# A seventh six-row group, one more sum by accumulating DMA, and a new written-out order in a WaveNet layer

## The chip, the cores and the metric

The kernel runs on one core of one Trainium2 chip. The metric is device time in microseconds (us) of one execution; lower is better. Engines are named as the profile names them: PE (TensorE), PEld (its weight loads), DVE (VectorE), ACT (ScalarE), POOL (GpSimd) and SP (SyncE, here only a DMA queue).

## The reference

```python
B, T, D, K = (2, 16000, 256, 3)          # all bfloat16
dil, pad = 2, 4
xp = jnp.pad(x, ((0, 0), (pad, 0), (0, 0)))
h  = sum over i of einsum('btc,cd->btd', xp[:, pad-2*i : pad-2*i+T, :], w[i])   # i = 0, 1, 2; d = 512
f, g = h[..., :256], h[..., 256:]
return (tanh(f) * sigmoid(g)) @ w_o
```

A causal convolution of three taps, two time steps apart, maps 256 channels to 512. Half of these go through tanh, half through a sigmoid, and the product of the two goes through a 256x256 matrix.

## The kernel before, in words

**Groups.** Each batch's 16000 time steps are cut into groups. A group of J rows holds J*R consecutive steps, laid out as J rows of R columns, so that the steps that a tap combines lie in different rows. Except for the first group (640 steps, kind P, computed tap by tap in `direct`, L406) the convolution is done with fewer products than taps, on sums and differences of rows:

- a four-row group (kind B, J = 4, R = 256: 1024 steps) takes four products, on the operands `m` and `p` (the sums at minus and plus one), `d0` (zero) and `d3` (infinity);
- a six-row group (kind A, J = 6, R = 256: 1536 steps) takes five, on `u1`, `rm` and `rp` (minus and plus one), `r0` (zero) and `ri` (infinity). Each of the last four is made in two steps: DVE makes `e`, `f`, `u0`, `u2` from the input tile and `u3`, `uh`, `ud` from `u1`; then `rm` is `e` plus `u3`, `rp` is `f` plus `u1`, `r0` is `u0` plus `uh` and `ri` is `u2` plus `ud`, written over `e`, `f`, `u0` and `u2`.

The As and Bs are numbered through both batches (A0 to A11, B0 to B12). `N_A = (6, 6)` gives the number of six-row groups in each batch; four-row groups take the rest, the last of them (B12) with R = 160.

**Blocks.** A group is computed in four blocks, one for each 128 of the 512 features, and each product is two matmuls (256 channels in two halves) of 2*R columns. The blocks stand in one sequence of 100 slots (`seq`, L180 to L188): four Bs first, then As and Bs mixed evenly, then two Bs.

For a block, PE makes the first product (F) in a PSUM bank, ACT copies it out (`c`, L432), PE adds the second (for A: M, then L; for B: L), and DVE combines the copy and the bank: `h` (halfway, A only, after M), `a` into a second PSUM bank and `y` into SBUF (A only), L435. PE then adds the products at zero (Z) to the first bank and at infinity (I) to the second. ACT applies tanh or sigmoid to the first bank (`b`), to `y` (A only) and to the second bank (`a`), L475. So a block costs ACT three instructions for a B and four for an A, and DVE one and three. DVE multiplies tanh by sigmoid (`g`, L494); PE multiplies by `w_o` in pieces of four matmuls (P, L512); ACT, at the very end DVE too (`v`), empties each piece into `osb` (`e`), and SP stores it (L540).

**The order.** Nothing is scheduled by a compiler: `PLAN` writes it out, one text line for each slot, from line -1 to line 104. A line has four parts: PE's letters, ACT's letters, DVE's letters and operands, and POOL's work. PE's F and M in line k are for block k, L for block k-1, Z and I for block k-2. H and R in the last lines are the output matrix's two halves for the last group. Every engine works through its own part in order and waits at semaphores.

POOL's part is put ahead of the line's `a` on DVE. A token there is a quarter of an operand (`d0`, `d3`, `r0`, `ri`, L382), a piece of the weights of six-row groups (`wa`, L299), or a whole `rm` or `rp`. Marks (`'`) name an earlier DVE instruction that a quarter is held behind. `rm` and `rp` are not computed on POOL; POOL issues an accumulating DMA for each:

```python
BY_DMA = ("rm", "rp")
...
if name in BY_DMA:
    return nc.gpsimd.dma_start(out=G[name][:, :, :, :R], in_=b, accum_op=op)
```

Input tiles (`xt`, four buffers for each kind) come by transposing DMAs from SP's queue (L234). A load stands in that queue at the end of the plan line that lies 15 slots ahead of the group's first (21 ahead for As), behind the stores of the lines before it.

Of the kernel before, what the change touches and what calls it, by code (L numbers as in the profile page):

```python
# [10 lines left out]


PLAN = """
 |  | d0.0 m.0 d3.0 p.0 G | 
F D D | c w |  | 
F L D | c d | m.1 a p.1 G | wa.1' wa.3'
F L Z I | c b | d0.1 a | wa.5' wa.0
L P F Z I | a e b c | a | wa.6
Z I F L P | a b c | d3.1 d3.2 d0.2 g a | wa.2
F L Z I | a c b | u1.0 e.0 a | wa.4'  # L20
L F Z I P | a c b | uh.0 g m.2 a | wa.14' wa.7' wa.8'
L P F Z I | a e e e b c | a | 
Z F P L I | a c b | u0.0 p.2 d3.3 u3.0 g a | wa.10 r0.0
L F Z I P | a e b c | u2.0 a | 
I F Z P L | a c b | ud.0 m.3 u2.1 g f.0 a | ri.0' r0.0'
L P F Z I | a e c b | a | 
Z L F I P | a b e c e | d0.3 u1.2 p.3 g f.1 a | rm.0 wa.15'
F L P Z I | a c b | d0.4 u1.1 d3.4 a | wa.12' wa.11
L F P Z I | a c e b e | a u3.1 m.4 g | wa.9
L Z F I P | a b c | u0.1 a | rp.0 r0.0'  # L30
F Z L I | a c b e | e.1 p.4 u3.2 a m.5 g | wa.13'
L F I Z P M | a c b | ud.1 a h | rm.1 r0.0' ri.0
F P Z L P I M | a e c e e b | g f.2 a y h | ri.0' ri.0 ri.1
F P Z L I | a e y b c | uh.2 u0.2 a y | d0.5' d3.5'
F L I Z M P | a c y b | uh.1 e.2 a h | r0.1' r0.2'
F I L Z M P | a c e e b | g a y h | rp.1 ri.1 r0.1
F Z L I | a y b c | g u2.2 a y | ri.1' d3.5'
F L I Z M P | c a y b | u1.3 ud.2 a h | r0.1' d0.5'
F Z L I M | a c b e | g a y h | rp.2 r0.1 ri.1
P F Z L I | a e y b c | e.3 ud.3 a y | rm.2 d0.5' d3.5  # L40
F L I Z M | a c y b | a p.5 h | d0.5 ri.2
Z I F L | a b c | g f.3 a y | r0.2' ri.2' d3.5'
F L P M P Z I P | c a e y b e e | g a h | ri.2
F L Z P M I | c a b e e | uh.3 u1.4 y u3.3 a h | ri.2' r0.2'
F Z L I P | a b c y | u3.4 u0.3 a y | d3.6' r0.2'
F L P Z I M | a e c b y | f.4 a g h | d0.6'
F I Z L P M P | c a b e | u2.3 uh.4 a y h | rp.3 rp.4 ri.3'' ri.3 d0.6''
F P Z L I | a e y e b c | g u0.4 a y | rm.3 d3.6' d3.6'
F P P Z L M I | a c e b e y | g m.6 a h | ri.3' r0.3
F Z L I | a b c | ud.4 e.4 a y | r0.3' ri.3'  # L50
F P L M Z I | c a y b | e.5 a h | d3.6' r0.3'
Z F I L P P M | a e b c e e e | u1.5 g p.6 a y h | rm.4 d0.6' r0.3' d0.6'
F P Z P L I | a c b y | g u2.4 a y | r0.4' ri.4 r0.4'
F L I Z M | a c y b | a m.7 h | ri.4
I F Z L P M P P | a e c b e | u0.5 g a h y | ri.4 d0.7
F L Z I P | a e e c b y | u3.5 a y | ri.4' d0.7'
F Z L I M | a c b y | e.6 uh.5 f.5 a h | d0.7' r0.4
F Z L I M P | a c e b | g a y h | r0.4 r0.5
F Z I L P P P | a e y c b e e e | u1.6 g a y | rp.5 d3.7
F L Z I M P P | a c y b | u3.6 u2.5 p.7 a h | r0.5' d0.7  # L60
Z F L I | a e b c | ud.5 g uh.6 a y | rm.5 ri.5' ri.5 r0.5'
F L I Z M P | a c e y b | f.6 a h | r0.5
Z F L I P M | a e b c e e | u0.6 u2.6 a y h | ri.5' ri.5'' d3.7''
F Z I L | a b c y | u1.7 g ud.6 a y | rm.6 d3.7' ri.6' d3.7' ri.6
F P L P M Z I | c a e y b | a h g | 
Z L F P I M P P | a c e e b e | f.7 a y h | rp.6 d3.8' d0.8' d3.8
Z P L F I | y a b c | u2.7 e.7 ud.7 a y | d0.8' r0.6''
F P L Z P M I | a e c y b e e | u3.7 g uh.7 a h | ri.7' r0.6'
F Z L P I | a b c e | u1.8 m.8 a y | r0.6' ri.6
F I L Z M P | a c y b | u0.7 g a h | rp.7 ri.6 d0.8 r0.6  # L70
F Z L M P I | a c b e e e | g a y h | ri.7 r0.7
F I Z L P | a c b y | u3.8 e.8 a y | d3.8
F P L Z M I | a c e b y | p.8 a h | rm.7 r0.7' d3.8'
F Z L P P M I | a e c b e e | u0.8 g a y h | ri.7 d0.8 r0.7 d0.9
F Z L I | a c b y | g a y | ri.7
L F I Z M P P | a c y b | f.8 uh.8 a h | rm.8 d3.9 d0.9'' r0.8'' r0.7''
F L P P M Z I | a e c e e e b | g y a h | d3.9
Z I L F | y b a c | u2.8 f.9 ud.8 y a | ri.8
F P L Z I M P | c y a b | e.9 u1.9 a h | ri.8' r0.8''
F Z L I | a c e b | g a y | rp.9 rp.8  # L80
L P F Z P M I | a c b y e | g u3.9 a h | r0.8' d3.9'
F I L Z M P | a c e b e | ud.9 u2.9 a y h | r0.8 ri.8'' d0.9''
I Z P L F | a e b y c | u1.10 uh.9 u0.9 a y | ri.8 d3.9 r0.9 r0.9
F P P L M Z I | c a e e b y | m.9 a h g | rm.9
Z F P L I P M | a c e b | f.10 a y h | d0.10' d0.9' ri.9'
F Z P L I | a y c b e | g p.9 a y | rp.10 r0.9' r0.9
F L I Z M | a c e b y | a ud.10 h u2.10 g | ri.9 d0.10
I F Z L P | a c b e e | a y | ri.9
L F P P Z M I | c a b y | uh.10 e.10 a h | ri.10' ri.9''
F Z I L P P M | a c e b e | u0.10 g a y h | d3.10 r0.10 r0.10  # L90
F Z I L P | a y b c | g a y | ri.10 ri.10
F L I Z M | a e c y b | u3.10 a p.10 h | r0.10'
Z P F L P I M P | a e e c b e e | g a y u2.11 h | rm.10 r0.10 d0.10 ri.10
Z F P L I P | y a c b e e | e.11 u1.11 a y | 
F L I Z M | a c y b | ud.11 a u3.11 h | d3.10'
Z P F L I M P | a b c e | m.10 g a y h | ri.11 d0.11
# [8 lines left out]
F P Z P L I | y a c b e e | a y | 
F L P Z M I | c a b y | p.11 a h g | d3.11' d3.12'
F Z L I | a c b e | a y | d3.12 d0.11
L F P P Z I | a y c e b | p.12 a g | d3.11'
L Z P F I | a b e c | m.12 a g | d0.12'
F Z L P I P | a c e e e b | a |   # L110
Z L I F P P P | a b e c e e | a g | d0.12
F I L P Z P | a c E b | a v | d3.12
I Z L P F | a b c | a g v | 
F Z I L P P | a c e b | a | 
# [9 lines left out]
def kernel(  # L124
# [13 lines left out]
    B, T, D = x.shape  # L138
    K, _, D2 = w.shape
    P = 128  # L140
# [13 lines left out]


    LEAD, TRAIL = 4, 1
    N_A = (6, 6)
    groups, of_kind = [], {"P": [], "A": [], "B": []}

    def group(kind, b, t, R):  # L160
        of_kind[kind].append(len(groups))
        groups.append(dict(kind=kind, b=b, t0=t, R=R, J=ROWS[kind]))
        return t + ROWS[kind] * R

    for b in range(B):
# [194 lines left out]
        return ins  # L360

    ON_TOP = {"rp": "f", "rm": "e", "r0": "u0", "ri": "u2"}
    BY_DMA = ("rm", "rp")

    def pre(g, name, eng, qs=slice(0, 4), behind=None):
        G = groups[g]
        R = G["R"]
        op, factor, a, b = operand(g, name)
        if name not in G:
            if name in ON_TOP:  # L370

                G[name] = G[ON_TOP[name]]
            else:
                pool = {"m": pre_pool, "p": pre_pool, "u3": sum_pool, "uh": sum_pool, "ud": sum_pool, "d0": dif_pool, "d3": dif_pool}.get(name, dif_pool)
                G[name] = pool.tile([P, 2, CT, RG], bf16, name=name, tag=name)
        if name in BY_DMA:
            return nc.gpsimd.dma_start(out=G[name][:, :, :, :R], in_=b, accum_op=op)
        o, a, b = (t if t is None else t.rearrange("p q ct r -> p (q ct) r")[:, qs] for t in (G[name][:, :, :, :R], a, b))
        if op is None:
            ins = eng.tensor_scalar_mul(o, a, factor)  # L380
        else:
            ins = eng.tensor_tensor(out=o, in0=a, in1=b, op=op)  # L382
        return hold(ins, behind)
# [185 lines left out]
    def gpsimd(tokens):  # L569
        for token in tokens:  # L570
# [5 lines left out]
            g, name = group_of(token)  # L576
            if name in BY_DMA:
                pre(g, name, None)
# [153 lines left out]
```

## Time and profile before

| | |
|---|---|
| median of three runs | 265.5 us (265.42 to 265.58) |
| the profiled execution | 266.35 us |
| its span, first to last instruction | 264.5 us |
| PE busy | 259.1 us (98%) |
| ACT busy | 244.2 us (92%) |
| DVE busy | 238.8 us (90%) |
| POOL busy | 143.8 us (54%) |
| mean granted PE clock | 0.996 |

The profile shows the profiled execution, which took 1.85 us more than its span and 0.85 us more than the median. The number of instructions of a kind stands behind an x, the mean duration of one in ns behind the comma; consecutive instructions of an engine overlap, so that durations add up to more than the engine's busy time.

### The profile page before, as it was taken

Reading aid. Unit: us, or ns where it says so; the run is one execution under the profiler, and the core shown is the slowest. Engines: PE = TensorE matmul, PEld = TensorE weight load, DVE = VectorE, ACT = ScalarE, POOL = GpSimd, SP = SyncE. Lnnn points to the kernel's source line nnn. Section 1 sums busy time; section 2 is a strip of 40 time slices with the busy share of each in tenths; the row PEclk is TensorE's granted clock in tenths of the full one; section 3 lists DMA queues with packets and bytes.
Section 4 is the critical chain, followed back from the end, with each engine's and each line's share of the span. In section 5 each row is a group of like instructions: output and inputs, shape, how many; then the busy total and the mean of one; then the engine's idle time right before and its main releaser. Section 6 shows DMA issues by size and latency. Waiting matters only on the chain.

```text
span 264.5 us, 4509 instructions
## 1 busy us (share of the span) xinstructions
PE 259.1 (98%) x1476; PEld 143.9 (54%) x1476; DVE 238.8 (90%) x396; ACT 244.2 (92%) x487; POOL 143.8 (54%) x209
## 2 busy tenths in 40 slices
PE   8999999999999999999999999999999999999993
PEld 5655555544455555465565545555555555555682
DVE  2999999999999999999999999999999997788372
ACT  4889989999999999999999999899999999999993
POOL 1034346668768775567858755758566266523100
PEclk9999999999999999999999999999999999999998
DMA  6999979839916793769447999856346436120425
GB/s 189 221 167 215 260 132 203 222 76 215 247 60 142 166 228 91 193 157 234 137 105 182 227 146 230 180 133 149 99 118 165 97 86 175 59 79 0 162 99 188
DMA packets 79583, 41.25 MB, mean 156 GB/s; under 512 B 68648, under 2 KB 69928, under 8 KB 79560
## 3 DMA queue, kind: packets, MB, share of 16 engines
q1 hardware_dynamic: 75060, 33.66, 51.7%
q0 software_dynamic: 3456, 6.29, 14.5%
q10 hardware_dynamic: 1044, 1.02, 1.2%
q8 instruction: 11, 0.18, 0.3%
q14 instruction: 12, 0.10, 0.1%
HBM read 1.25 MB, written 16.38 MB: 67 GB/s over the span
## 4 chain that ended last, share of the span: by engine, by line
PE 96%; ACT 2%; issue 0%; ACTq 0%
PE b L401 56%; PE o_ps L512 20%; PE a L401 16%; PE b L421 1%; PE a L421 1%; PE a L216 1%; ACT osb L537 1%; ACT sg L475 1%; ACT ss L432 0%; PE fill L248 0%; PE tp L308 0%; ACT th L475 0%; ACTq L432 0%
## 5 line engine op out<-in xcount | busy, mean ns | idle before, releaser
L435 DVE SCALAR_TENSOR_TENSOR a<-ss,b 128x512 f32<-128x512 f32 (+1 forms) x100 | 67.9, 683 | 10.6 <-PE b L401 5.6
L512 PE MATMUL o_ps<-wo_sb,zz 128*128 128x256 bf16 x496 | 70.9, 273 | 0.0
L537 ACT CAST osb<-o_ps 128x512 bf16<-128x512 f32 x118 | 69.6, 629 | 0.6 <-PE o_ps L512 0.4
L432 ACT COPY ss<-b 128x512 f32<-128x512 f32 (+1 forms) x100 | 60.5, 607 | 6.3 <-PE b L401 4.9
L512 PEld LDWEIGHTS <-zz 128*128 128x128 bf16 x496 | 48.5, 98 | 26.2
L382 POOL TENSOR_TENSOR d<-xt 128x256 bf16<-128x256 bf16 (+1 forms) x64 | 42.3, 668 | 35.5 <-DVE zz L494 12.9
L401 PEld LDWEIGHTS <-w_sb 128*128 128x128 bf16 x400 | 39.0, 98 | 39.6 <-issue 1.0
L382 POOL TENSOR_TENSOR u<-u,ud 128x256 bf16<-128x256 bf16 x48 | 35.7, 748 | 29.5 <-DVE zz L494 19.8
L382 POOL TENSOR_TENSOR u<-u,uh 128x256 bf16<-128x256 bf16 x48 | 38.4, 806 | 14.4 <-DVE zz L494 8.1
L494 DVE TENSOR_TENSOR zz<-th,sg 128x1024 bf16<-128x1024 bf16 (+2 forms) x52 | 41.5, 797 | 0.6 <-ACT sg L475 0.5
L435 DVE SCALAR_TENSOR_TENSOR hh<-ss,b 128x512 f32<-128x512 f32 x48 | 32.8, 682 | 3.0 <-PE b L401 2.4
L435 DVE SCALAR_TENSOR_TENSOR yy<-hh,b 128x512 f32<-128x512 f32 x48 | 32.6, 679 | 0.6 <-PE b L401 0.5
L475 ACT ACTIVATE sg<-b 128x512 bf16<-128x512 f32 (+1 forms) x50 | 31.1, 622 | 2.3 <-PE b L401 1.8
L475 ACT ACTIVATE th<-b 128x512 bf16<-128x512 f32 (+1 forms) x50 | 31.0, 620 | 2.2 <-PE b L401 1.7
L475 ACT ACTIVATE th<-a 128x512 bf16<-128x512 f32 (+1 forms) x50 | 31.3, 625 | 0.3 <-PE a L401 0.2
L475 ACT ACTIVATE sg<-a 128x512 bf16<-128x512 f32 (+1 forms) x50 | 31.3, 627 | 0.0
L401 PE MATMUL a<-d,w_sb 128*128 128x512 bf16 (+1 forms) x104 | 30.3, 373 | 0.0
L401 PE MATMUL b<-d,w_sb 128*128 128x512 bf16 (+1 forms) x104 | 30.3, 373 | 0.0
L401 PE MATMUL b<-m,wm_sb 128*128 128x512 bf16 (+1 forms) x104 | 30.1, 373 | 0.0
L401 PE MATMUL b<-p,wp_sb 128*128 128x512 bf16 (+1 forms) x104 | 30.1, 373 | 0.0
L401 PEld LDWEIGHTS <-wp_sb 128*128 128x128 bf16 x200 | 19.5, 98 | 19.1 <-issue 0.7
L401 PEld LDWEIGHTS <-wm_sb 128*128 128x128 bf16 x200 | 19.5, 98 | 16.8 <-issue 0.4
(57 smaller groups left out, 339.4 us busy)
## 6 DMA issues: line engine op xcount, KB each, us to landing
out_dram<-osb SPq DMA_DIRECT2D x24, 384.0 KB, 2.5
out_dram<-osb SPq DMA_DIRECT2D x26, 256.0 KB, 2.5
e<-u POOLq DMA_DIRECT2D x12, 256.0 KB, 4.3
f<-u POOLq DMA_DIRECT2D x12, 256.0 KB, 4.0
w_sb<-in_w_dram ACTq DMA_DIRECT2D x3, 256.0 KB, 4.0
xt<-in_x_dram SPq DMA_TRANSPOSE x25, 5.6
xn<-in_x_dram SPq DMA_DIRECT2D x1, 160.0 KB
xn<-in_x_dram ACTq DMA_DIRECT2D x1, 160.0 KB, 4.3
```

The costliest lines, as they stand in the source:

```text
L216: nc.tensor.matmul(wps[:], lhsT=ones[:, 0:P], rhs=ones, start=True, stop=True,)
L382: ins = eng.tensor_tensor(out=o, in0=a, in1=b, op=op)
L401: nc.tensor.matmul(G[bank, oi][:, :2 * R], lhsT=wmat[:, ct, osl], rhs=G[mv][:, :, ct, :R], start=which == "first" and ct == 0, stop=ct == ...
L421: nc.tensor.matmul(G[bank, oi][:, :4 * r].rearrange("p (j r) -> p j r", j=4), lhsT=w_taps[tap][:, ct, osl], rhs=xt[:, j0:j0 + 4, ct, c0 + ...
L432: nc.scalar.copy(out=G["ss", oi][:, :n], in_=G["b", oi][:, :n])
L435: return note(nc.vector.scalar_tensor_tensor(out=out, in0=in0, scalar=scalar, in1=in1, op0=ALU.mult, op1=op))
L475: nc.scalar.activation(out=G[name, dt][:, j:j + 2, :R], in_=G[bank, oi][:, :2 * R].rearrange("p (q r) -> p q r", q=2), func=(ACT.Tanh, ACT ...
L494: note(nc.vector.tensor_tensor(out=G["z"][:, dt, :, :n], in0=G["th", dt][:, :, :n], in1=G["sg", dt][:, :, :n], op=ALU.mult))
L512: nc.tensor.matmul(o_ps[:, q, :], lhsT=z, rhs=wo_sb[:, dt, :], start=dt == 0 and (q == 0 or len(dts) == NT), stop=dt == NT - 1, skip_group ...
L537: copy(out=osb[:, 2 * jp:2 * jp + 2, :], in_=o_ps[:])
```

## The change

```diff
-    N_A = (6, 6)
+    N_A = (6, 7)
...
-    BY_DMA = ("rm", "rp")
+    BY_DMA = ("rm", "rp", "r0")
```

In the second batch there are seven six-row groups (A0 to A12 in all). Four full four-row groups are left there instead of six, followed by one with R = 160 (B10, as B12 was) and a last one with R = 128 (B11). `r0` is made by an accumulating DMA, one for each group, instead of four quarters on POOL. The whole of `PLAN` is replaced. In the new one `m` and `p` of four groups, B5 to B8, are made by quarters on POOL instead of on DVE; the number of lines is the same (106). The counts of the tokens:

| | before | after |
|---|---|---|
| DVE: `a`, `h`, `y` | 100, 48, 48 | 100, 52, 52 |
| DVE: each of `u0 u1 u2 e f`, `u3 uh ud` | 12 | 13 |
| DVE: `m`, `p` | 13, 13 | 8, 8 |
| DVE: `d0`, `d3` | 5, 5 | 5, 5 |
| DVE: `v` (emptying pieces) | 6 | 4 |
| POOL quarters: `d0 d3`, `r0`, `ri`, `m p` | 64, 48, 48, 0 | 56, 0, 52, 32 |
| POOL's DMAs | 24 | 39 |

Lines of the new plan, with their numbers put ahead of them (the text after "SP:" tells which load the program puts at the end of line 52):

```text
52 F L P I M Z P | c a e y b | u1.8 a h | ri.6'               SP: load of B8
53 Z F I L P M | a b c e | u2.7 g a y h | d3.7 d0.7 p.8
54 P F Z P L I | a e y c b e e | g u3.7 ud.7 ud.8 uh.7 a y | rm.7 d3.7'' d3.7'' d3.7
55 F L P P M Z I | a c e e y b | a h | d3.8
56 Z L F I P M | a b c e | u0.8 u2.8 u3.8 a y h g | rp.7 p.8' ri.7 ri.8
...
63 L F Z I M | a c b | a y h | r0.8 ri.8 ri.8 d0.8
64 I Z F L | a y b c | u3.9 u2.9 a y | rp.9 m.8''
65 F P L I Z M | a c e y b | g a h | rm.9 m.8
```

The last lines, before and after:

```diff
-L Z I P p | a e b | g a v | 
-Z I P p P | a e b | v | 
-H H H | a e E | g v | 
-R R R |  |  | 
- | e E | v | 
+L Z I P | a e b | a g v | 
+Z I | a e b |  | 
+H H | a | g | 
+R R |  |  | 
+ | e | v | 
```

More of the change, by code (lines that the diff above doesn't have):

```diff
@@ L13 @@
 PLAN = """
- |  | d0.0 m.0 d3.0 p.0 G |
+ |  | p.0 m.0 d3.0 d0.0 G |
 F D D | c w |  |
[L16 to L36, printed above, removed]
@@ L105 @@
[L105 to L114, printed above, removed]
[L115 to L119 removed]
+F L D | c d | m.1 a G | wa.6
@@ new lines @@
+F L Z I | c b | a | wa.4
+L Z P F I | a b c | p.1 d0.1 a | wa.0'
+Z F L I | a b c | d3.2 d3.1 g a | wa.2
+F L Z I | a c b | u2.0 a | wa.1
+L Z I F P | a b e c | m.2 u1.0 a d0.2 ud.0 g | wa.3
+Z F I L | a b c | f.0 a | ri.0 wa.12'
+F P L Z I | a c e b e | p.2 a g | rp.0
+L F Z P I | a c b e | d0.3 a | wa.14
+L Z I F P | a b c | d3.3 u3.0 e.1 g a | wa.7
+F P L I Z P | a c e e b e | e.0 u1.1 a | wa.5'
+L P P Z I F P | a e e b c | uh.0 m.3 u2.1 > u0.1 a p.3 g | rm.0 wa.13'
+Z L F I | a b c | uh.1 d3.4 a | ri.0'
```

154 lines of the change are left out of this document (86 added, 68 removed).

## The prediction

> **What bounds the kernel now.** I read the page first, for the shares of the span and the chain that ended last.
>
> ```profile
> span 264.5 us, 4509 instructions
> ...
> PE 259.1 (98%) x1476; PEld 143.9 (54%) x1476; DVE 238.8 (90%) x396; ACT 244.2 (92%) x487; POOL 143.8 (54%) x209
> ...
> DMA  6999979839916793769447999856346436120425
> ...
> q0 software_dynamic: 3456, 6.29, 14.5%
> ...
> PE 96%; ACT 2%; issue 0%; ACTq 0%
> ```
>
> PE is 96% of the chain, but ACT and DVE are nearly as full. A busy PE need not be a PE at its pace, so the second view is the chain in order of time, which gives the pace, and the third the groups by shape, which give the number of matmuls.
>
> ```profile
> 5.28 3.08 PE b L421 x18
> ...
> 14.09 1.29 PE b L401 x6
> ...
> 58.18 1.46 PE b L401 x6
> ...
> 62.73 1.46 PE b L401 x6
> ...
> 248.24 1.31 PE o_ps L512 x12
> ```
> ```profile
> 255.31 0.54 PE b L401 x4
> ```
> ```profile
> L512 PE MATMUL o_ps<-wo_sb,zz 128*128 128x256 bf16 x496 | 70.9, 273 | 0.0
> ...
> L401 PE MATMUL b<-m,wm_sb 128*128 128x512 bf16 x96 | 28.5, 379 | 0.0
> ```
>
> An undisturbed matmul of 512 columns takes 1.29/6 = 0.215 us, one of 256 columns 1.31/12 = 0.109, one of 320 columns 0.54/4 = 0.135. There are nine groups of 96 like the second one here (864, 185.8 us), 500 of 256 columns (54.5) and 80 of 320 (10.8): 251.1 us. PE starts on real work at 5.28 us and issues its last matmul at about 259.8, so only some 3 us in 254.5 are not matmuls at full pace: 0.65 of it in the first 18 (3.08 instead of 2.43), and most of the rest in waits like those at 58.18 and 62.73, which make a run of six 0.17 us longer. PE's number of columns sets the time. The fourth view asks how near the others are, by stage.
>
> ```profile
> core 0: us, PE busy (x) PEld busy (x) DVE busy (x) ACT busy (x) POOL busy (x), PEclk, DMA share, GB/s
> ...
> 14.00:56.00 42.00, 42.00 (x228) 22.09 (x227) 41.58 (x74) 38.40 (x76) 21.44 (x32) 1.00 0.93 185
> 56.00:100.00 44.00, 43.91 (x240) 23.31 (x239) 43.66 (x74) 42.07 (x83) 32.64 (x44) 1.00 0.82 175
> ...
> 220.00:246.00 26.00, 26.00 (x147) 14.14 (x145) 19.69 (x31) 25.02 (x51) 10.39 (x18) 1.00 0.23 77
> 246.00:264.50 18.50, 13.95 (x110) 10.48 (x107) 8.74 (x18) 13.51 (x31) 0.90 (x2) 0.94 0.37 140
> ```
>
> DVE is full until 100 us (43.66 of 44, 0.59 us an instruction) and slack at the end; ACT is the second engine at the end (25.02 of 26, 0.49 us an instruction). POOL has room everywhere.
>
> **The change part by part: PE.** Two full four-row groups go: 2 x 4 products x 4 blocks x 2 halves = 64 matmuls of 512 columns, 13.76 us. A six-row group comes, 5 x 4 x 2 = 40 of them, 8.60 us, and the four-row group of R = 128, 32 matmuls of 256 columns, 3.49 us by the output product's pace. Steps and output product stay the same. Sum: **-1.67 us**, on the path that sets the end.
>
> **The end.** After the last block's product at infinity PE must wait for ACT's last activation and DVE's last gate before it can do R. These rows show the chain before.
>
> ```profile
> 257.11 0.43 PE L401 MATMUL a<-d,w_sb 128*128 128x320 bf16 x2
> ...
> 257.38 1.47 PE L512 MATMUL o_ps<-wo_sb,zz 128*128 128x256 bf16 x12
> ...
> 257.70 0.43 ACT L475 ACTIVATE sg<-a 128x320 bf16<-128x320 f32 x1
> ...
> 258.31 0.42 DVE L494 TENSOR_TENSOR zz<-th,sg 128x512 bf16<-128x512 bf16 x1
> ...
> 259.98 0.59 ACT L537 CAST osb<-o_ps 128x512 bf16<-128x512 f32 x1
> ```
>
> From the start of that product (257.11) to the end of the gate (258.73) 1.62 us pass, and PE is covered: three pieces (12 matmuls) and the H halves stand behind it. In the new plan only H H stands behind `Z I` in line 101: the product itself 0.22 and four matmuls 0.44, 0.66 us. Narrower tiles shorten the chain to an estimated 1.4 us (the odd piece's gate goes, each step has 256 instead of 320 columns), which leaves a hole of 0.74; ACT has an `e` ahead of the last two activations in each of lines 100 and 101, for which I add 0.15. **+0.9 us**, bounds 0.4 (nothing added, shorter steps) and 1.6 (both evictions, 0.59 each, half uncovered). After the last matmul one store remains instead of two; I cost that at nothing, since both were under way together.
>
> **DVE.** Durations overlap, so I use the pace of 0.59 and take shorter tiles off by the difference of these rows.
>
> ```profile
> L435 DVE SCALAR_TENSOR_TENSOR a<-ss,b 128x512 f32<-128x512 f32 x96 | 65.9, 691 | 8.0 <-PE b L401 4.6 <-ACT sg L475 2.3 <-ACT th L475 0.2
> ...
> L380 DVE TENSOR_SCALAR ud<-u 128x1024 bf16<-128x1024 bf16 x12 | 5.1, 426 | 0.0
> ...
> L435 DVE SCALAR_TENSOR_TENSOR a<-ss,b 128x320 f32<-128x320 f32 x4 | 2.0, 494 | 2.6 <-ACT th L475 1.5 <-PE b L401 1.0
> ```
>
> Four more `h` and `y`: +4.7. Four `a` become short (0.2 less or more each): -0.8. Operands of a group more: five at 0.59, three at 0.33 (426 against 691 ns): +3.9. `m` and `p`: ten fewer, -5.9, two shorter, -0.4. Two `v` fewer: -1.2. Gates: even. Sum +0.3 in 238.8, and by the plan's counts the surplus comes late, where DVE is slack; in the full first 100 us, where `m.5` to `p.6` leave it, it has about 1 us more room than before. I count nothing for that; it is worth at most the 2 us of waits that are there.
>
> **ACT.** Eight full blocks of three give way to four of four and four short ones of three, and two pieces come from DVE: -24 + 16 + 2 = -6 instructions of 0.49 us, and 12 short ones at an estimated 0.3: +0.7 us. Behind ACT's room in the page (20 us) that is nothing; at the end, where it has 1 us in 26, it comes off the rest: by counting, lines 83 to 104 hold as much ACT work as PE work, where before ACT had over 3 us less. Bounds 0 and +1 us beside the hole above; I take 0, because ACT at 25.02 of 26 cost PE nothing there (26.00 of 26.00).
>
> **POOL and the DMAs.**
>
> ```profile
> L382 POOL TENSOR_TENSOR d<-xt 128x256 bf16<-128x256 bf16 x56 | 38.6, 696 | 23.0 <-DVE zz L494 7.0 <-DVE yy L435 6.8 <-DVE e L382 3.2
> L382 POOL TENSOR_TENSOR u<-u,uh 128x256 bf16<-128x256 bf16 x48 | 38.4, 806 | 14.4 <-DVE zz L494 8.1 <-DVE u L382 4.5 <-DVE uh L380 0.7
> L382 POOL TENSOR_TENSOR u<-u,ud 128x256 bf16<-128x256 bf16 x48 | 35.7, 748 | 29.5 <-DVE zz L494 19.8 <-DVE yy L435 4.7 <-DVE u L382 3.4
> ...
> L494 DVE TENSOR_TENSOR zz<-th,sg 128x1536 bf16<-128x1536 bf16 x24 | 22.9, 952 | 0.0
> ...
> L377 POOL DMA_DIRECT2D e<-u x12 | 10.5, 877 | 0.0
> ```
> ```profile
> DMA to landing us min/median/max: 3.3/4.2/5.6
> ```
>
> POOL loses 48 quarters of `r0` (38.4 us, the second row) and 8 of `d` (5.6), and gains 32 of `m` and `p` (0.70 each, 22.3), four of `ri` (3.0) and 15 issues (0.88 each, 13.2): -5.5 us, and it sits off the path. What matters is lateness. An accumulating DMA landed 3.3 to 5.6 us after its issue (the last line is the view of the line that issues them). By the plan the shortest way from PE's start of a line with `r0` to the matmul that reads it is 5.6 us (`r0.8`: line 63, 2.15; line 64, 1.72; F, a piece, L and I of line 65, 1.73); the next are 6.1 (`r0.3`) and 6.5. So typical landings are covered and only the longest is not. Price 0, bounds 0 and +1. The queue q0 goes from 14.5% to 14.5 x 39/24 = 23.6% of the DMA engines; they are at 0.93 in the stretch from 14 to 56 us, but only two of the 15 DMAs fall there.
>
> A rule of the Trainium skill speaks against this part: by "SBUF — State Buffer", section "SBUF: two separate sides", GpSimd cannot write a DMA's descriptors while DVE holds the port that they share, so that such a DMA seems blocked. The DMAs here were issued beside a DVE that was 98 to 99% busy, and landed in 3.3 to 5.6 us; if that holds for the new ones the rule is in the numbers already.
>
> **Sum.** -1.67 + 0.9 = -0.77 us: 266.35 becomes 265.6 for a profiled execution. Carried to the median shown, which lies 0.85 lower, 265.5 becomes **264.7 us**.
>
> **The rivals.** *More room* (15%): PE's waits in the middle go, since DVE has the room, and the hole at the end is at its lower bound: -1.67 + 0.4 - 0.7 = -2, 263.5 us. For it: the waits are short and DVE was full where they are. Against: the plan is another, and brings its own.
>
> *Nothing gained* (14%): ACT, without room in the last 40 us, delays copies and banks by another 0.7 us: 265.4.
>
> *Late loads hold POOL* (25%), the one that ends slower. The load of B8 stands at the end of line 52, and `p.8`, which reads it, in line 53; B10 (line 77, read in 78) and B7 (39, read in 41) are like it.
>
> ```profile
> 147.66 2.27 SPq L234 DMA_TRANSPOSE xt<-in_x_dram  x1
> ```
> ```profile
> DMA to landing us min/median/max: 3.6/5.6/9.0
> ```
>
> The rows are the nearest load before, of B9, which stands in line 56 and was first read in line 59, and the landings of all (the view of the tile `xt`). POOL works in order: while `p.8` waits, `rm.7`, three quarters of `d3.7` and `rp.7` wait behind it. From the end of line 52, PE reaches the product that reads `d3.7` after line 53 (2.6 us), line 54 (2.6), line 55 (3.0) and three products (1.3): 9.5 us. POOL needs 0.7 + 0.9 + 2.1 = 3.7 after the landing, so a landing later than 5.8 us after line 52 decides. With the median of 5.6 it just does; with the longest PE waits 3.2 us. SP may issue earlier, because the last store ahead of that load belongs to line 50; that is why I do not take this as likeliest. Two such places at about 1 us: -0.77 + 2 = +1.2, 266.7 us.
>
> *Late sums* (4%): the skill's rule as a mechanism: an issue is held for one more gate, 0.95 us (952 ns above), on top of the longest landing, 6.6 us, and `r0.8`, `r0.3` wait 1.0 and 0.5: -0.77 + 1.5 = +0.7, 266.2 us. No landing in the profile speaks for it.
>
> **How the numbers follow.** A measurement of this kernel can tell about 0.2%, 0.5 us, from no change: below 265.0 is faster, above 266.0 slower. The forecast has 42%; within its own bounds (hole 0.4 to 1.6) it reaches from 264.2 to 265.4, and about a fifth of that I put within 0.2%. Faster: 34 + 15 = 49%. Same: 8 + 14 = 22%. Slower: 25 + 4 = 29%. The range goes from the "more room" case with 1 us of the waits gone, 263.2, to the late loads with 2.3 us at their places, 267.0.
>
> **What would show it.** Right: PE has 1476 - 64 + 72 matmuls (1484) and the same pace; a hole of near 1 us on PE ahead of the last four matmuls, ended by DVE's gate; no `u<-u,uh` on POOL and 39 DMAs that land in under 6 us; DVE near 239 us, ACT near 245, POOL near 138. Wrong: POOL idle for microseconds ahead of a `p` or `d` and released by a load, with PE's waits in the products behind; waits of PE on DMAs at Z of an A block; or runs of six matmuls that take over 1.29 us all through the last 40 us, released by ACT.

## The result and the profile after

The changed kernel takes **269.2 us** (median of four runs, 267.8 to 274.5) against 265.5 us on the same chip (265.3 to 265.6): ratio **1.0106, 95% interval 1.0079 to 1.0133**. It is slower by about 1.1%; 264.7 was forecast. The profiled execution took 268.24 us, its span 266.5 against 264.5. Ratios here leave out runs over 1.5% above a kernel's fastest; since late transfers make some runs of the changed kernel longer than that, I give the spread of all runs beside them.

The page of the kernel after, the lines that answer to those of before:

```profile
span 266.5 us, 4558 instructions
...
PE 257.4 (97%) x1484; PEld 143.5 (54%) x1484; DVE 243.4 (91%) x400; ACT 245.0 (92%) x493; POOL 140.1 (53%) x204
...
q0 software_dynamic: 5616, 10.23, 23.5%
...
PE 84%; ACT 6%; DVE 5%; issue 2%; ACTq 1%
```

The counts are as forecast (1484 matmuls, 23.5% for the queue, ACT 245.0). Two things are not: DVE is busy for 243.4 us instead of 239, and the chain that ended last went from 96% PE to 84%, with DVE and ACT in the gap. The view of PE's waits (what was waited for: us in total, times, longest) held only the warm-up line (`PEq`) for the kernel before. Now it has these:

```profile
PE b L401 <- DVE yy L435: 1.3, 2, 1.2
PE a L216 <- PEq L716: 0.8, 1, 0.8
PE b L401 <- DVE hh L435: 0.7, 1, 0.7
PE o_ps L512 <- DVE zz L494: 0.7, 1, 0.7
PE b L401 <- ACT ss L432: 0.7, 1, 0.7
PE a L401 <- DVE a L435: 0.5, 1, 0.5
```

`o_ps` waiting for `zz` is the forecast hole at the end. The other waits for DVE and ACT are new. From the starts of all matmuls and their undisturbed pace (0.2159, 0.1360 and 0.1093 us for 512, 320 and 256 columns), the two spans compare so: PE reaches the plan's first product at 10.93 us instead of 11.81 (-0.88); the matmuls from there on are worth 244.67 us instead of 246.36 (-1.69; forecast -1.67); waits among them come to 6.61 us instead of 1.61 (+5.00); from the end of the last matmul to the end of the span it is 4.24 us instead of 4.74 (-0.50). Sum +1.93, the measured difference. The first of these differences is not the change's: in the other profiles below the first product comes at 10.8 to 11.9 us with the new plan and at 11.1 to 11.4 with the old one.

Of the 6.61 us, 0.85 is the hole at the end, 0.83 a wait at 37.5 us that begins with a store, and about 4.4 lie between 50 and 180 us, 3.1 of it in four waits that DVE ends (at 66.6, 80.3, 148.0 and 173.8 us).

**Where DVE lost time.** The timeline of the kernel after around line 54 (start, duration; DVE, then POOL, then PE):

```profile
144.01 0.76 DVE L380 TENSOR_SCALAR ud<-u 128x1024 bf16<-128x1024 bf16 x2
144.68 2.10 DVE L380 TENSOR_SCALAR uh<-u 128x1024 bf16<-128x1024 bf16 x1
146.71 0.68 DVE L435 SCALAR_TENSOR_TENSOR a<-ss,b 128x512 f32<-128x512 f32 x1
...
144.40 0.88 POOL L377 DMA_DIRECT2D e<-u  x1 [1.32 <-DVE u L380]
145.01 1.48 POOL L382 TENSOR_TENSOR d<-xt 128x256 bf16<-128x256 bf16 x2
...
148.03 0.59 PE L401 MATMUL b<-u,w_sb 128*128 128x512 bf16 x2 [1.16 <-DVE yy L435]
```

`uh.7` takes 0.42 us elsewhere and 2.10 here. Behind `rm.7` POOL has run two quarters of `d3.7`, and DVE stands still until both are over; `a` and `y` come late, and PE waits 1.3 us for `y`. The Trainium skill says on the page "SBUF — State Buffer", section "SBUF: two separate sides", that DVE and GpSimd share a port pair as an exclusive lock, which goes to whichever starts first "for the whole instruction". The trace agrees that one waits for the whole of the other; who came first is less plain, since by the records `uh.7` starts 0.33 us ahead of the first quarter (144.68 against 145.01).

Five more places are like it. DVE took 1.93 us instead of 0.95 for `g` of line 24, 1.76 instead of 0.67 for `u2.9` (line 64), 1.2 instead of 0.7 for `u0.2` (19), for `g` and for `u1.4` (29), 1.34 instead of 0.94 for `g` (30). Over all DVE instructions, what they took beyond the shortest of their form (where that is over 80 ns) sums to **6.1 us; before, 1.3** (the expectations below count one of them less, 5.6). All of them read and write SBUF alone. `a`, `h` and `y`, which read PSUM, were never longer by more than 26 ns, though most of them ran beside a quarter; and of some 35 SBUF operations that overlapped only the issue of a DMA, the worst lost 0.15 us.

What POOL is doing as the DVE operation starts decides who pays. In the three largest places (`uh.7`, `u2.9`, `g` of line 24) POOL was issuing a sum at that moment, here `rm.7` from 144.40 us, with a quarter queued right behind. Over all 17 profiles 50 DVE operations lost more than 0.2 us, and each of them started while POOL had a quarter or a piece of the weights (35) or such an issue (15) under way. In 397 cases in which POOL was at none of these and a quarter started during the operation, DVE lost at most 0.02 us, and in most of them the quarter grew instead.

**Where the transfers lost time.** Answers on the tiles `xt` and `f` of the kernel after (the load issued at 25.4 us, `rp.0` at 26.1 us, and the landing of each behind its issue), and the wait on ACT that followed:

```profile
L234 SPq DMA_TRANSPOSE xt<-in_x_dram x1: 4236/4236/4236, 25.4 to 25.4; - x1
...
DMA to landing us min/median/max: 9.3/9.3/9.3
```
```profile
L377 POOL DMA_DIRECT2D f<-u x1: 1004/1004/1004, 26.1 to 26.1; - x1
...
DMA to landing us min/median/max: 8.4/8.4/8.4
```
```profile
35.34 1.07 ACT L537 CAST osb<-o_ps 128x512 bf16<-128x512 f32 x2 [0.85 <-DMA out_dram<-osb]
```

Before, sums landed in 3.3 to 5.6 us. Here the load and the first sum both took over 8 us, the next store came late behind them, and ACT waited for that store's buffer. The new plan issues `rp.0` in line 8 instead of line 15.

### The profile page after: what moved, and what is told of

Its sections match the earlier page's. It is cut to its first block, busy times and chain, and to the rows that moved or that the text cites. A ratio compares the mean times of both kernels' runs of the same rounds, so it can differ in the third digit from the quotient of the medians.

```text
span 266.5 us, 4558 instructions
## 1 busy us (share of the span) xinstructions
PE 257.4 (97%) x1484; PEld 143.5 (54%) x1484; DVE 243.4 (91%) x400; ACT 245.0 (92%) x493; POOL 140.1 (53%) x204
## 3 DMA queue, kind: packets, MB, share of 16 engines
q0 software_dynamic: 5616, 10.23, 23.5%
## 4 chain that ended last, share of the span: by engine, by line
PE 84%; ACT 6%; DVE 5%; issue 2%; ACTq 1%
PE b L401 50%; PE o_ps L512 17%; PE a L401 14%; ACT sg L475 2%; ACT th L475 2%; ACT osb L537 1%; PE b L421 1%; PE a L421 1%; DVE a L435 1%; ACT ss L432 1%; DVE hh L435 1%; DVE zz L494 1%; DVE yy L435 1%; ACTq L256 1%; ACT L267 0%
## 5 line engine op out<-in xcount | busy, mean ns | idle before, releaser
L435 DVE SCALAR_TENSOR_TENSOR a<-ss,b 128x512 f32<-128x512 f32 (+2 forms) x100 | 67.0, 671 | 10.7 <-PE b L401 5.4
L432 ACT COPY ss<-b 128x512 f32<-128x512 f32 (+2 forms) x100 | 59.2, 593 | 5.1 <-PE b L401 4.2
L382 POOL TENSOR_TENSOR d<-xt 128x256 bf16<-128x256 bf16 (+2 forms) x56 | 34.2, 626 | 37.2 <-DVE zz L494 24.4
L494 DVE TENSOR_TENSOR zz<-th,sg 128x1536 bf16<-128x1536 bf16 (+2 forms) x52 | 42.8, 823 | 0.8 <-ACT sg L475 0.5
L401 PE MATMUL b<-u,w_sb 128*128 128x512 bf16 x104 | 30.9, 379 | 1.4 <-DVE yy L435 1.3
L401 PE MATMUL b<-f,wp_sb 128*128 128x512 bf16 x104 | 30.9, 379 | 0.7 <-DVE hh L435 0.7
L401 PE MATMUL a<-u,w_sb 128*128 128x512 bf16 x104 | 30.9, 379 | 0.5 <-DVE a L435 0.5
L401 PE MATMUL b<-u,wa_sb 128*128 128x512 bf16 x104 | 30.9, 379 | 0.0
L475 ACT ACTIVATE sg<-a 128x512 bf16<-128x512 f32 (+2 forms) x50 | 30.9, 618 | 0.0
L401 PE MATMUL b<-e,wm_sb 128*128 128x512 bf16 x104 | 30.9, 378 | 0.0
```

The source lines that it names most:

```text
L401: nc.tensor.matmul(G[bank, oi][:, :2 * R], lhsT=wmat[:, ct, osl], rhs=G[mv][:, :, ct, :R], start=which == "first" and ct == 0, stop=ct == ...
L432: nc.scalar.copy(out=G["ss", oi][:, :n], in_=G["b", oi][:, :n])
L435: return note(nc.vector.scalar_tensor_tensor(out=out, in0=in0, scalar=scalar, in1=in1, op0=ALU.mult, op1=op))
L475: nc.scalar.activation(out=G[name, dt][:, j:j + 2, :R], in_=G[bank, oi][:, :2 * R].rearrange("p (q r) -> p q r", q=2), func=(ACT.Tanh, ACT ...
L494: note(nc.vector.tensor_tensor(out=G["z"][:, dt, :, :n], in0=G["th", dt][:, :, :n], in1=G["sg", dt][:, :, :n], op=ALU.mult))
```

## The experiments

Each ratio is to the kernel before on the same chip in the same batch. Its median there was 266.2 us for experiments 1 to 4, 266.1 for 5 to 8, 266.3 for 9 to 12 and 266.4 for 13 to 15, not the 265.5 of the first comparison; so ratios can be compared across batches, and times less well.

My theory after this: (A) quarters that meet DVE's SBUF operations cost some 4 us; (B) the early sum beside a load costs 0.8 us and more, by chance. Rivals: the denser mix of six-row groups is too much for DVE by itself; the sums by DMA are dear in themselves.

### First four

**1. Quarters moved away from DVE's SBUF operations.** Fifteen lines of POOL's part, no other:

```diff
18 -r0.1 ri.0' ri.1 d3.5' ri.1 ri.1' m.5       +r0.1 ri.0' ri.1 d3.5'
19 -                                           +ri.1'' ri.1'
21 -rp.1 p.5                                   +rp.1 p.5 m.5
24 -rm.2 p.5                                   +rm.2
26 -                                           +p.5'
28 -rm.3 m.5 ri.2 ri.3 d0.5 ri.3               +rm.3 m.5 ri.2 ri.3
29 -ri.2'                                      +ri.2 d0.5
30 -d3.5' d3.6' m.6'                           +d3.5'' d3.6'
31 -ri.3                                       +ri.3 ri.3
32 -d0.6'                                      +d0.6' m.6
54 -rm.7 d3.7'' d3.7'' d3.7                    +rm.7 d3.7 d3.7
55 -d3.8                                       +d3.7 d3.8
64 -rp.9 m.8''                                 +rp.9 m.8
69 -ri.9 d3.9 d0.9                             +ri.9 d3.9
70 -                                           +d0.9
```

> Only 15 lines of POOL's part of the new plan differ: quarters that ran beside a VectorE operation that reads and writes SBUF alone are put beside its PSUM operations, one or two lines later or with fewer marks. All counts, PE's, ACT's and VectorE's parts stay. Theory (a GpSimd quarter and a VectorE operation on SBUF shut each other out): the sum of what VectorE's operations take over the shortest of their kind falls from 5.6 us to under 1.5, VectorE's u from xt goes back from 743 to about 690 ns, PE's waits at 65, 80, 148 and 174 us go, and 3.5 to 4.3 us are won: profiled about 264.3, below the kernel before. Rival (the denser mix of six-row groups is too much for VectorE by itself): VectorE still 243 us busy, PE still waits 4 us in the first 180 us, 268. Rival (more traffic by accumulating DMAs): no change, 268.

Measured: 268.6 us (266.9 to 271.2), ratio 1.0087 (1.0056 to 1.0118). DVE's excess fell from 6.1 to 0.8 us, its busy time to 238.7, and none of the waits at 65, 80, 148 and 174 us is left; but the time hardly moved. Three views of its profiled execution (271.2 us) show why: the timeline, PE's granted clock (the whole span in 40 slices) and the DMA engines (19 us from 26 us on in 40 slices):

```profile
41.64 1.01 PE L401 MATMUL b<-p,wp_sb 128*128 128x512 bf16 x2 [3.94 <-ACT ss L432]
42.45 1.06 PE L401 MATMUL b<-m,wm_sb 128*128 128x512 bf16 x2
...
46.71 0.81 PE L401 MATMUL b<-d,w_sb 128*128 128x512 bf16 x2
47.36 0.59 PE L401 MATMUL a<-d,w_sb 128*128 128x512 bf16 x2
```
```profile
PEclk9999995999999999999999999999999999999999
```
```profile
DMA  9999996699999999999999999799999999679999
GB/s 249 236 285 247 116 45 31 31 185 287 223 39 39 158 63 74 161 73 120 121 77 149 58 146 66 169 397 385 276 233 213 350 311 323 175 167 118 85 200 182
```

The load took 12.8 us to land and `rp.0`, issued 0.4 us behind it, 11.8; in several slices the DMA engines count as 60% busy or more while 31 to 45 GB/s pass. The stores came late, ACT waited, PE stood still for 4.1 us, and for the 5 us after that each matmul took twice its time (1.06 us a pair instead of 0.59, starts 0.43 apart instead of 0.22), about 2.8 us more. On that the Trainium skill ("TensorE: Matmul & The Clock Gate", Part 1: "The HAM clock gate") says that an idle window of about 3.4 us halves the array's clock until such a window has been busy; the rows agree, with half the pace behind a wait of 4.1 us, though it lasted 5 us. So the harm of (B) was not 0.8 us in this run but near 7.

**2. The kernel before with `r0` by DMA, alone.** In `before`, for each of the 12 groups:

```diff
-    BY_DMA = ("rm", "rp")
+    BY_DMA = ("rm", "rp", "r0")
10 -ri.0' r0.0'                                +ri.0'
...
```

> The kernel before with one part of the change alone: each r0 by one accumulating DMA, issued where the first of its four quarters stood; the other 36 tokens are taken out. PE's, ACT's and VectorE's work stays. Theory (the harm is in where quarters lie beside VectorE, and the DMAs are in time): 265.4 within 1 us, POOL down by 28 us (48 quarters of 0.81 less 12 issues of 0.88), the queue's share at 22%, and whatever PE loses lies where a VectorE operation on SBUF meets a quarter. Rival (the DMAs' traffic or lateness): slower by 2 us or more, with PE's waits at the products at zero ended by DMAs, or with later landings of loads and stores.

Measured: 271.6 us (267.4 to 273.7). This went the rival's way. The profiled run (273.7) shows one place, the tiles `u` and `xt` at 28 us, and PE's waits:

```profile
L377 POOL DMA_DIRECT2D u<-uh x1: 1007/1007/1007, 28.1 to 28.1; - x1
...
DMA to landing us min/median/max: 11.5/11.5/11.5
```
```profile
PE b L401 <- DVE p L382: 4.4, 1, 4.4
PE b L401 <- DVE hh L435: 1.1, 1, 1.1
```

`r0.0` is issued 0.24 us behind a load; they land after 11.5 and 11.9 us, DVE's `u1.2` waits for that load with `p.3` queued behind it, PE waits 4.4 us for `p.3` and runs at half pace after it. At 100.3 us the same happens (`rm.4` 0.23 us behind a load, 9.1 and 9.7 us; PE waits 1.1). The rival's word "dear in itself" is not settled by this: experiment 9.

**3. A piece moved into the hole at the end.**

```diff
 99 -F I Z L P P        +F I Z L P
101 -Z I                +Z I P
```

> The kernel after with one piece (four matmuls of 256 columns) moved in PE's part from line 99 to the end of line 101, so that it stands between the last products and the last eight matmuls. Theory (a hole of 0.85 us before the last four matmuls): the hole shrinks by the piece's 0.44 us and the end comes 0.3 to 0.45 us earlier, 267.8 profiled. Rival (ACT has no room at the end, so a later piece only delays the last evictions): no gain or 0.3 us slower.

Measured: 273.9 us (272.7 to 275.9). Much of this is the early wait again (3.2 us at 40.6 in the profile, and half pace), which this edit has nothing to do with; one run was profiled, and why all six are long is not known. The end is read from the trace alone, and the rival is right:

```profile
265.86 0.39 ACT L475 ACTIVATE sg<-b 128x256 bf16<-128x256 f32 x1
...
267.04 0.61 PE L512 MATMUL o_ps<-wo_sb,zz 128*128 128x256 bf16 x4 [1.05 <-DVE zz L494]
```

The piece is finished later, its eviction on ACT stands ahead of the last two activations, and the hole grows from 0.85 to 1.22 us.

**4. A fourth output buffer.**

```diff
+    osb4_pool = ctx.enter_context(tc.tile_pool(name="osb4", bufs=4))
-            G["osb", rb0] = osb_pool.tile(...
+            G["osb", rb0] = (osb4_pool if J == 4 else osb_pool).tile(...
```

> The kernel after with a fourth buffer for the four-row groups' output tiles (osb), nothing else. Theory (ACT waited 0.85 us at 35 us for an older store to land, and PE lost 0.83 us at 37.5 us behind it): both waits go and the end is 0.8 us earlier, 267.4. Rival (the wait only covers another one, VectorE's collisions behind it absorb the gain): the wait goes, the waits of the next 20 us grow by as much, no change.

Measured: 269.7 us (267.3 to 274.5), ratio 1.0123 (1.0095 to 1.0152). The profiled run (267.28) has neither wait, and its span is 1.0 us shorter than that of the kernel after; but there the load and `rp.0` landed after 7.2 and 4.7 us, so the buffer was not put to the test, and other runs are as long as without it. Inconclusive.

### Second four: the place of the first sum

**5. The kernel before with its first sum early.**

```diff
 8 -wa.10 r0.0          +wa.10 r0.0 rm.0
12 -rm.0 wa.15'         +wa.15'
```

> The kernel before with one token moved: its first accumulating DMA (rm.0) is issued in line 8 instead of line 12, at about 29.4 us, so that it is under way together with the transposing load issued at 28.25. Theory (an accumulating DMA and a transposing load under way together can hold each other up): both land more than 8 us after their issue instead of 4.0 and 6.0, PE stands still for 2 to 4 us before 45 us and runs at a lower granted clock behind it, and the runs scatter by more than 2 us; median 268 to 272. Rival (two transfers share the engines and nothing more): landings up to 7 us, no wait of PE over 0.5 us, 265.5 to 266.5 and no scatter.

Measured: 267.0 us (266.4 to 268.9) beside 266.1 (265.7 to 267.2): 1.0035 (1.0017 to 1.0053). Slower, but less than the theory said. `rm.0` went out 1.6 us behind the load, not 0.2 to 0.7 as the first sums of experiments 1 to 3 and of the kernel after; they landed after 5.4 and 7.2 us, and PE waited 0.4 and 0.25 us for DVE near 40 us. Overlap as such was cheap here; that pointed to the distance from the load's issue.

**6. The kernel after with its first sum late.**

```diff
 8 -rp.0                +
12 -rm.0 wa.13'         +rm.0 rp.0 wa.13'
```

> The kernel after with one token moved: the first accumulating DMA (rp.0) is issued in line 12, at about 33.4 us, instead of line 8, at 26.1 us, behind the landing of the load issued at 25.4 us. Theory (that overlap makes the long waits and the scatter): the load lands in under 7.5 us, no PE wait over 0.3 us between 30 and 45 us, runs within 1 us of each other, 267.2; what is left over 264.7 are VectorE's collisions. Rival (the scatter has another source, the denser plan or the new r0 sums): runs still from 267 to 274.

Measured: 268.1 us (267.8 to 268.7), ratio 1.0071 (1.0048 to 1.0094). The spread goes from 6.7 us to 0.9, and no run is long. The load landed after 6.1 us, no wait is left between 15 and 50 us, and DVE's excess is still 5.6 us. Theory B holds for the scatter. The median is 0.9 us above the theory's 267.2; the profile has a PE wait of 0.9 us at 14.8 us, behind a DVE that waited for a load, which the profile of the kernel after does not have.

**7. Both: the edits of 1, 4 and 6.**

> The kernel after with both: rp.0 issued in line 12, the quarters beside VectorE's SBUF operations moved as in the first experiment, and the fourth output buffer for four-row groups. Theory (the two causes are the whole loss): 4.3 us and 0.8 us won against the profiled kernel after, PE's waits after the head at most 2.5 us of which 0.85 at the end, span 261.5 to 262.5, 263.3 to 264.3 profiled, runs within 1 us: faster than before by 0.6 to 1.0%. Rival (the mix itself is dearer, or collisions come back elsewhere): 266 or more.

Measured: **264.6 us** (264.2 to 266.2), ratio **0.9949** (0.9925 to 0.9973): faster than before, by a little less than the theory's 0.6%; the span (262.9) and the profiled run (264.66) lie 0.4 us above its ranges, and the runs spread over 2.0 us. Its profile has a PE wait of 1.1 us near 15 us, of the kind just named. The same place as above, with the quarters behind `uh` (four of them, 2.36 us, beside `a`, `y` and `a`):

```profile
143.19 0.55 DVE L381 TENSOR_SCALAR uh<-u 128x1024 bf16<-128x1024 bf16 x1
143.66 0.68 DVE L436 SCALAR_TENSOR_TENSOR a<-ss,b 128x512 f32<-128x512 f32 x1
...
142.90 0.92 POOL L378 DMA_DIRECT2D e<-u  x1 [1.31 <-DVE u L381]
143.83 2.36 POOL L383 TENSOR_TENSOR d<-xt 128x256 bf16<-128x256 bf16 x4
```

**8. Three of the places put back.**

```diff
24 -rm.2                +rm.2 p.5
26 -p.5'                +
54 -rm.7 d3.7 d3.7      +rm.7 d3.7'' d3.7'' d3.7
55 -d3.7 d3.8           +d3.8
64 -rp.9 m.8            +rp.9 m.8''
```

> The run before this one in the list with three of the moved places put back as the kernel after has them: p.5 right behind rm.2 in line 24, three d3.7 with their marks in line 54, m.8 with its marks in line 64. Theory: VectorE's g of line 24, uh.7 of line 54 and u2.9 of line 64 take 1.0, 1.7 and 1.1 us longer again, PE waits about 1.05, 1.3 and 0.75 us behind them, and the end is 2.5 to 3.1 us later than without. Rival (VectorE's room absorbs them): the operations are longer, the end at most 0.5 us later.

Measured: 267.5 us (266.7 to 268.6), **2.9 us** more than 7 on the same chip; ratio 1.0044 (1.0025 to 1.0063). The three operations took 0.99, 1.68 and 1.09 us longer, to 0.01 us what they did in the kernel after, and PE waited 0.89, 1.32 and 0.75 us. Theory A is shown: 3.8 us on DVE become 2.9 in the time. All three tokens put back stand right behind the issue of a sum. The three operations:

```profile
63.89 1.93 DVE L495 TENSOR_TENSOR zz<-th,sg 128x1536 bf16<-128x1536 bf16 x1
...
143.92 2.10 DVE L381 TENSOR_SCALAR uh<-u 128x1024 bf16<-128x1024 bf16 x1
...
170.65 1.76 DVE L383 TENSOR_TENSOR u<-xt 128x1024 bf16<-128x1024 bf16 x1
```

### Third four: what is left

**9. Experiment 2 with four DMAs elsewhere.**

```diff
 8 -wa.10 r0.0          +wa.10
12 -rm.0 wa.15'         +r0.0 rm.0 wa.15'
25 -rm.2 d0.5' d3.5     +d0.5' d3.5
26 -d0.5 ri.2           +rm.2 d0.5 ri.2
31 -d0.6'               +r0.3 d0.6'
34 -ri.3' r0.3          +ri.3'
37 -rm.4 d0.6' d0.6'    +d0.6' d0.6'
38 -r0.4 ri.4           +rm.4 r0.4 ri.4
```

> The second experiment's kernel (the kernel before, each r0 by one accumulating DMA) with four DMAs issued at another place: r0.0 with rm.0 in line 12 instead of 8, rm.2 in line 26 instead of 25, rm.4 in line 38 instead of 37, r0.3 in line 31 instead of 34; in the second experiment they were issued 0.2 to 1.2 us behind a transposing load, or landed late behind one. Theory (a sum issued in the first microsecond behind a load holds both up, and the DMAs cost nothing else): these land in under 7 us, PE has no wait over 0.5 us that a DMA ends, 265.8 to 266.6 with runs within 1.5 us. Rival (r0 by DMA is dear in itself, by traffic or by lateness): 267.5 or more.

Measured: 266.8 us (266.0 to 267.1) beside 266.3: 1.0017 (1.0004 to 1.0030). Moving four tokens took 4.9 us away (271.6 on another chip); `r0.0` lands after 3.4 us. One long wait is left, for DVE:

```profile
PE b L401 <- DVE hh L435: 0.7, 1, 0.7
```

It stands behind a `p` of 1.92 us instead of 0.68 that met quarters moved up by the edit. So what `r0` by DMA costs in itself is at most the 0.5 us that are left, and that wait would account for them; where it is issued costs ten times as much.

**10. A shorter end, on 7.**

```diff
100 -L Z I P | a e b    +L Z I | a b
101 -Z I | a e b        +Z I P | a b
102 -H H | a            +H H | a e e
```

> The seventh experiment's kernel with another end: ACT's last two evictions of pieces stand behind its last activation (lines 100 and 101 lose their e, line 102 gets two), and the odd piece (two matmuls) follows the last products on PE. Theory (the hole at the end hangs on ACT's evictions ahead of its last activations): the last gate ends 0.3 to 0.45 us earlier against PE's last product, the end comes 0.3 to 0.4 us earlier than the seventh experiment's, 264.2. Rival (ACT has no other work there, but PE waits for the evictions' banks): no gain.

**11. Experiment 7 again,** on the same chip as 10:

> The seventh experiment's kernel again, beside the two that are compared with it: 264.6, 0.3 to 0.8% faster than before.

Measured: 264.6 us (263.9 to 266.1; ratio 0.9939, 0.9918 to 0.9961) and 264.8 us (264.2 to 266.3; 0.9944, 0.9924 to 0.9965). The hole is shorter, but not for the theory's reason:

```profile
257.89 0.61 PE L513 MATMUL o_ps<-wo_sb,zz 128*128 128x256 bf16 x4 [0.40 <-DVE zz L495]
```

It is 0.56 us instead of 0.85. Most of that is the odd piece, which now stands in it (two matmuls, 0.22 us); the last gate ends 1.36 us after the start of PE's last product instead of 1.44, so that the evictions are worth 0.08 us there, not 0.3 to 0.45. PE waits 0.32 instead of 0.10 us one product earlier. The gain of 0.2 us in the median is within the uncertainty.

**12. Three output buffers, otherwise as 7.**

> The seventh experiment's kernel without the fourth output buffer. Theory (with rp.0 issued later the stores land in time): no wait of ACT for a store before 45 us, the same time as with four within 0.3 us. Rival (the buffer is what took the 0.83 us away): ACT waits 0.5 us or more for a store between 33 and 40 us, and the time is 0.5 to 0.9 us longer.

Measured: 264.6 us (264.1 to 266.2), ratio 0.9942 (0.9924 to 0.9961), and ACT waits for no store before 45 us: the buffer is not needed. This kernel differs from the one after in POOL's part of the plan alone. Its page:

```profile
span 262.6 us, 4557 instructions
...
PE 256.5 (98%) x1484; PEld 143.7 (55%) x1484; DVE 238.6 (91%) x400; ACT 244.3 (93%) x493; POOL 137.3 (52%) x204
...
PE 97%; ACT 1%; DVE 1%; issue 0%; ACTq 0%
```

DVE is at 238.6 and POOL at 137.3, what the prediction gave them. The groups of DVE, of the kernel after and of this one (count, busy us, mean ns, idle):

```profile
L494 DVE TENSOR_TENSOR zz<-th,sg 128x1536 bf16<-128x1536 bf16 (+2 forms) x52 | 42.8, 823 | 0.8 <-ACT sg L475 0.5
...
L382 DVE TENSOR_TENSOR u<-xt 128x1024 bf16<-128x1024 bf16 x39 | 28.7, 743 | 0.1
...
L380 DVE TENSOR_SCALAR uh<-u 128x1024 bf16<-128x1024 bf16 x13 | 7.3, 558 | 0.0
```
```profile
L494 DVE TENSOR_TENSOR zz<-th,sg 128x1536 bf16<-128x1536 bf16 (+2 forms) x52 | 41.0, 789 | 0.8 <-ACT sg L475 0.5
...
L382 DVE TENSOR_TENSOR u<-xt 128x1024 bf16<-128x1024 bf16 x39 | 27.0, 700 | 0.4 <-DMA xt<-in_x_dram 0.4
...
L380 DVE TENSOR_SCALAR uh<-u 128x1024 bf16<-128x1024 bf16 x13 | 5.6, 430 | 0.0
```

These three fell by 1.8, 1.7 and 1.7 us of busy time; `a`, `h` and `y` are the same in both kernels to 0.1 us. So the denser mix is not too much for DVE: that rival falls. Quarters and SBUF operations still meet: 56 of the 124 full quarters overlap one here, 63 in the kernel after. What went are the meetings that DVE paid for.

### Last three: overlap, or the moment of issue

Each is experiment 12 with `rp.0` taken out of line 12: **13** has it in line 8 (the kernel of experiment 1), **14** in line 9 (`wa.14 rp.0`), **15** in line 10 (`wa.7 rp.0`).

> The twelfth experiment's kernel (the kernel after without VectorE's collisions, rp.0 issued in line 12) with rp.0 back in line 8, as the kernel after has it, 0.3 to 0.7 us behind a load; the first experiment's kernel again. Both readings: 267 to 271, with a wait of PE of 1 us or more before 45 us.

> The same with rp.0 issued in line 9, about 28.2 us, 1.3 to 2.3 us behind that load, which is still under way. Theory A (what counts is that the sum is issued in the first microsecond behind the load): the load lands in 6 to 7.5 us, the sum in under 6, no wait of PE for it, 264.4 to 265.2. Theory B (any overlap of the two does it): both land after 8 us or more, 266.5 to 270.

> The same with rp.0 issued in line 10, about 30.9 us, 4 us behind the load and 2 us ahead of its landing. Theory A: 264.4 to 265, as with line 12. Theory B: a shorter overlap, landings of 6 to 8 us, 265 to 267.

| | all runs, us | median | ratio | `rp.0` behind the load's issue | load, sum landed after |
|---|---|---|---|---|---|
| 13, line 8 | 264.0 to 271.6 | 267.7 | 0.9954 (0.9929 to 0.9980) | 0.42 us | 11.6, 10.7 us |
| 14, line 9 | 263.8 to 265.9 | **264.2** | **0.9925** (0.9903 to 0.9948) | 2.09 us | 7.7, 5.5 us |
| 15, line 10 | 264.1 to 266.2 | 264.4 | 0.9935 (0.9913 to 0.9956) | 5.48 us | 6.5, 3.8 us |

Line 8 has two kinds of runs: five of twelve at 264.0 to 265.5, as if nothing were wrong, and seven at 267.5 to 271.6. One of the seven was profiled and none of the five, so what sets these apart is not known. One line later, with the load still under way, none of six runs is long, nor with the sum in line 10: theory A of these, the moment of issue. `rp.0` in the profiles of 13 and 14:

```profile
L377 POOL DMA_DIRECT2D f<-u x1: 1002/1002/1002, 27.1 to 27.1; - x1
...
DMA to landing us min/median/max: 10.7/10.7/10.7
```
```profile
L377 POOL DMA_DIRECT2D f<-u x1: 1151/1151/1151, 29.0 to 29.0; - x1
...
DMA to landing us min/median/max: 5.5/5.5/5.5
```

The profiles of all kernels here point the same way. By how far a sum was issued behind the load before it:

| behind the load | sums | landed after, median (longest) | over 7 us |
|---|---|---|---|
| under 0.2 us | 21 | 4.8 us (9.7) | 1 |
| 0.2 to 0.7 us | 14 | 7.6 us (11.8) | 10 |
| 0.7 to 1.5 us | 39 | 5.8 us (11.3) | 5 |
| 1.5 to 3 us | 67 | 5.5 us (7.0) | none |
| over 3 us | 486 | 3.9 us (9.5) | 5, all queued behind a pair held up |

These are not 627 independent cases: the same few places return in many kernels, and all 21 under 0.2 us lie at 43, 73 to 76 and 200 to 209 us. The table supports the reading, and experiments 13 to 15 carry it. The bad stretch is from 0.2 to about 1.2 us rather than the whole first microsecond.

Experiment 14 has the lowest median, 0.75% under the kernel before; 12 and 15 are not told from it by their intervals. What in the transfers makes that stretch special stays open.

## Why the prediction was wrong, point by point

**The step that failed is DVE's cost.** It took the pace of 0.59 us for every operation and got +0.3 us; in the kernel after, the same operations took 6.1 us beyond their shortest (1.3 before), nearly all of it beside POOL's quarters. PE's waits between 50 and 180 us came to 4.4 us, of which experiment 12, without these collisions, keeps 0.7. The step looked at POOL's total (138 us, "off the path") and at lateness, never at which DVE operation each of the new `m`, `p` and moved `d`, `ri` quarters would meet, though the lock between the two engines, whose rule it cites, is about just that. It weighed that rule for the DMAs only, and closed with "the rule is in the numbers already". (The DVE busy share of 98 to 99% that it names there holds to 180 us; from 180 to 220 us it was 95%.) For the landing of the sums that held. For DVE it held for the old plan's 1.3 us, not for the new plan. Experiments 8 (2.9 us for three places) and 6 against 12 (which differ in nothing else: ratios 1.0071 and 0.9942, 3.4 us) show the size.

**The second step that failed is the DMAs.** It priced the time from a sum to its own reader, and there it was right: every sum landed at least 1.1 us ahead of its use. It wrote that only two of the 15 new DMAs fall into the crowded stretch, and passed over that `rp.0`, an old one, moves from line 15 to line 8, just behind a load. What came too late was not the sum for its reader but the load and the stores beside it. The price is 0.8 us in the profiled run, near 7 in that of experiment 1, and 3.5 in the median between experiments 13 and 14.

**What held.** Columns: -1.67 forecast, -1.69 in the trace. The hole: 0.9 forecast, 0.85 found, released by DVE's gate. The chain from PE's last product to the end of the gate took 1.44 us (1.4 estimated); the 0.15 added for ACT's evictions is not borne out, as experiment 10 finds 0.08 at most. The end behind the last matmul, costed at nothing, gave 0.5 us back, in every profile of the new plan. ACT (245), POOL in experiment 12 (137.3 against 138) and the queue (23.5 against 23.6%) are as worked out. Without the two missing costs the kernel takes 264.2 to 264.8 us (experiments 7, 11, 12, 14, 15). That this lies at the forecast 264.7 is luck: beside the kernel before on the same chips it is 1.4 to 2.2 us less, where the sum had -0.77. So a plan that places its quarters and its first sum otherwise does gain, and by more than the sum says: the 0.5 us at the end are part of that, and the rest no run takes apart.

**The rivals.** *Late loads hold POOL*, the one on the slow side, pointed the right way for the wrong reason, and not far enough (+1.2 us, where the median moved by 3.7): the load of B8 was issued at 135.6 us and `p.8` did not wait for it; of its three places only B10's cost POOL a wait for a load, 0.46 us at 209 us, and PE none. *Late sums*: no sum was late for its reader. *Nothing gained*: PE's waits in the last 20 us, the hole apart, come to 0.2 us. *More room*: its -2 us is what experiment 14 reaches (0.75%, 2.0 us), by other terms. None of the rivals was DVE held up by POOL, which the prediction should have had as the slow one.

## What to carry to other kernels

Before moving work to GpSimd, list what VectorE runs at that moment: beside operations that read PSUM a quarter of 0.65 us is free, beside those in SBUF it is paid by one side or the other. In these traces VectorE paid only where GpSimd was already at work as its operation started, most of all on a DMA issue with a quarter queued right behind. Such an issue also shifts the quarter out of its place. When a plan is rewritten, go through the DMAs that merely moved, and see what else is in flight when each is issued; here runs that suddenly scattered came from two transfers that met, and a median of four runs does not show such a thing.

## What the runs showed of the hardware that was not expected

- A VectorE operation with a single SBUF input (`uh`, 0.42 us) was held for 1.68 us by two GpSimd instructions in a row: it did not get in between them. GpSimd was issuing a DMA as it started. Where a quarter started during a VectorE operation in SBUF and GpSimd had been at no other work of its part of the plan (397 cases), VectorE lost at most 0.02 us, and the quarter took 0.99 us in the median instead of 0.65 (1.39 instead of 0.61 us at 183.6 us in the kernel after, beside a gate).
- An accumulating DMA issued 0.2 to 0.7 us behind a transposing load landed after 7 to 12 us in 10 of 14 cases, the load with it, in one of them at 31 to 45 GB/s with the DMA engines counted 60% busy or more.
- PE's wait of 4.1 us (experiment 1) was followed by some 5 us at half pace, one of 3.2 us (experiment 3) by 3 us of it, and one of 3.45 us (experiment 13) by none. So in these runs the length of the wait alone did not decide it.
